# Routed experts behind sliding-window attention: gather buffers on the other side, one store per block of rows, two lists of ids, logits of six heads ahead, expert 0 by slabs

## The chip, the cores and the metric

One core of one Trainium2 chip runs the whole kernel in one launch. The metric is device time in microseconds. The core's engines run each its own list of instructions and wait for each other by semaphores: PE (TensorE, matmuls; PEld are its weight loads), DVE (VectorE), ACT (ScalarE), POOL (GpSimd) and SP (SyncE, which here only issues transfers). Transfers run on 16 DMA engines that all queues share.

## The reference

Attention with a sliding window of 96 and 8 global positions (4 batches, 8 heads, 768 positions, head size 64), then a layer of 8 experts in which each expert takes exactly 384 of the 3072 tokens:

```python
keep = is_global | is_local                 # is_local: 0 <= rel < 96
scores = where(keep, q @ k.T / 8 - slope * dist, -1e9)
x = softmax(scores) @ v                     # -> (3072 tokens, 512)
logits = x @ w_gate                         # (3072, 8)
for idx in argsort(-logits.flatten()):      # best pair first
    tok, e = idx // 8, idx % 8
    if assigned[tok] < 0 and counts[e] < 384:
        assigned[tok] = e; counts[e] += 1
for e in range(8):
    h = maximum(x[assigned == e] @ w1[e], 0)
    out[assigned == e] = h @ w2[e]
```

## The kernel before

*Attention.* Heads go in pairs (`n`, 16 of them) and the steps of a pair are laid out by the table `ORDER`, whose rows give a step and how many rounds it lags. `sums` leaves on PE, for a pair, the row sums and the product with the gate's weights. `sums_out` (LT) transposes that on DVE and takes reciprocals, `gates_out` (GT) scales it into `Gb` (six chunks x 8 heads x 8 experts of a batch) and `logits_out` (LS) adds the eight heads into `L_sb`, the logits: 128 partitions x 24 chunks x 8 experts. The last batch's `logits_out` is one reduction on DVE, after the last pair.

*Token rows.* `tok_in` turns attention output round on PE, `tok_out` scales it (on ACT, four activations a piece, or on DVE) into a tile `x`, and when a tile is full SP stores it to `x_tok` in DRAM (L493), in four transfers of 32 partitions: the rows of `x_tok` stand in the order of the tokens, and a chunk's 128 partitions are four groups of 32 tokens that lie 192 apart. Most of these pieces run inside the routing, between its steps.

*Routing.* In a `manual_schedule` block, where instructions stand in the order in which they are written, four rounds (`fast_round`) refine which expert each token goes to. Each begins in `best` with the minimum over the experts for all chunks (`mn`) and a comparison with it (`nb`). GpSimd issues one weight transfer a round (`late_weights`). `dispatch` then makes, for each place 0..3071 of the experts' lists, the token's id: masks `OH` and `ohl` on DVE, 24 matmuls into `pI` in four groups of six, and two DVE steps into `idi`. Between the groups and behind them stand `fill` matmuls, whose product nobody reads. Last, `pf`, `fc8`, `fm` and `fi` find whether any expert has more than 384 tokens; a branch at the end of the program would then take a slow path.

*Experts.* For expert e, `gather` fetches the rows of its 384 tokens from `x_tok` by `idi`, as three indirect transfers of GpSimd (128 rows each, tiles `xe`). `load_x` transposes a slab of 128 tokens on PE and copies it on DVE into `xT`; 32 matmuls of 384 columns and 8 activations on ACT give `hT`; 24 matmuls of 512 columns give the result, which DVE copies to `ot` and GpSimd scatters to `out` by `idi` (L1055). Gathers run two experts ahead. GpSimd's queue also carries the weights of experts 2 to 7: four transfers (1 MB each as stored) during the routing, the other eight in the loops of experts 0 to 3, two each.

*Memory.* The attention's token tiles (`tokp`) lie on the right side of the on-chip memory. The routing's pools are opened on the left side, the first of them `dap`, which holds `fc8` and `fm`. When they are closed, the experts' pools take the same place, the first of them `gp`, with the gather buffers `xe` and the weights of experts 6 and 7. The tile framework makes the first use of a place wait for the last use of what lay there.

Line numbers of the quoted kernel are those of the profile. Around the change the order comes from the written order inside `manual_schedule`, and behind it from the framework's scheduler, except where `keep_in_program_order` pins an instruction.

Of the kernel before, what the change touches and what calls it, by code (L numbers as in the profile page):

```python
# [42 lines left out]
def kernel(  # L43
# [46 lines left out]
    idc = consts.tile([128, NCHUNK], FP16)  # L90
    idn = consts.tile([128, NCHUNK], FP32)
# [74 lines left out]
    def _():  # L166
        nc.gpsimd.memset(Lb[:, 0:8, :], 0.0)
# [11 lines left out]
    Lb = lpool.tile([128, 32, N_EXP], FP32)  # L179
    L_sb = Lb[:, 8:32, :]  # L180
# [21 lines left out]
    with ExitStack() as actx:  # L202
# [214 lines left out]

        def sums_out(n):
# [46 lines left out]
        def tok_out(piece, xpool, eng):  # L465
# [44 lines left out]
        def step(op, u):  # L510
# [37 lines left out]
            elif k == "LT":  # L548
                sums_out(n)
# [6 lines left out]
            elif k == "GT":  # L556
                gates_out(n, nc.vector if last else nc.gpsimd)
            elif k == "LS":
                if u % 2 == 1:
                    logits_out(u // 2, nc.vector if last else nc.gpsimd)  # L560
# [104 lines left out]
    idi = consts.tile([128, NCHUNK], I32)  # L665
    fi = consts.tile([1, 1], I32)

    def routing(general):
      with ExitStack() as dctx:
# [16 lines left out]
        mn = rpool.tile([128, NCHUNK], FP32, tag="mn", name="mn")  # L686
        turn = rpool.tile([128, 1], FP32, tag="turn", name="turn")
        nb = rpool.tile([128, 256], BF16, tag="nb", name="nb")
# [30 lines left out]
        def best(X, Dg):  # L719
            if X is None:  # L720
                UB = Lb
            else:
# [6 lines left out]
            nc.vector.tensor_reduce(out=mn, in_=UB[:, 8:32, :], axis=AX.X, op=ALU.min)  # L729
            return UB  # L730

        def fast_round(kk, k, X, Dg):
# [7 lines left out]
            nc.vector.tensor_tensor(out=nb[:, 64:256].rearrange("p (c e) -> p c e", e=N_EXP),  # L740
                                    in0=UB[:, 8:32, :], in1=bc_e(mn), op=ALU.is_gt)
# [65 lines left out]
        def dispatch():  # L807
# [34 lines left out]
            nc.vector.tensor_tensor(out=OH, in0=OH, in1=bc_m(idc, NCHUNK), op=ALU.mult)  # L842
            pI = ps_d.tile([128, NCHUNK], FP32, tag="rk", name="pI")
# [269 lines left out]
```

## Time and profile before

| | |
|---|---|
| median of 3 runs | 276.59 us (276.26 to 277.07) |
| the profiled execution | 275.88 us, its span 274.1 us |
| busy: PE, DVE, ACT, POOL | 233.4 (85%), 148.8 (54%), 152.5 (56%), 153.3 (56%) us |
| mean granted TensorE clock | 0.944 of full speed |
| transfers | 49.22 MB, mean 180 GB/s |

Times in rows are microseconds from the span's start. A row of the timeline gives start, duration, engine, line, operation, output<-input, and in brackets how long the engine stood idle before it and what ended that. A row with xN merges N instructions. PE's busy time counts matmuls as the profiler models them. The DMA share is the mean busy share of the 16 engines, and overlapping packets can take it over 1.

### The profile page before, as it was taken

Reading aid. Unit: us, or ns where it says so; the run is one execution under the profiler, and the core shown is the slowest. Engines: PE = TensorE matmul, PEld = TensorE weight load, DVE = VectorE, ACT = ScalarE, POOL = GpSimd, SP = SyncE. Lnnn points to the kernel's source line nnn. Section 1 sums busy time; section 2 is a strip of 40 time slices with the busy share of each in tenths; the row PEclk is TensorE's granted clock in tenths of the full one; section 3 lists DMA queues with packets and bytes.
Section 4 is the critical chain, followed back from the end, with each engine's and each line's share of the span. In section 5 each row is a group of like instructions: output and inputs, shape, how many; then the busy total and the mean of one; then the engine's idle time right before and its main releaser. Section 6 shows DMA issues by size and latency. Waiting matters only on the chain. (4 is left out here: it accounts for less than half of the span.)

```text
span 274.1 us, 6678 instructions
## 1 busy us (share of the span) xinstructions
PE 233.4 (85%) x2633; PEld 162.5 (59%) x2633; DVE 148.8 (54%) x324; ACT 152.5 (56%) x296; POOL 153.3 (56%) x281
## 2 busy tenths in 40 slices
PE   0678599999998999998778792599999999999960
PEld 0666478888887888886666430355565555655520
DVE  3699688979898965644878810212323223333130
ACT  2549569898989898563788910053251341522500
POOL 6888637486959899855120004826675555741240
PEclk9995599999999999999999997599999999999995
DMA  7999967585472599951999941499999999530321
GB/s 246 351 347 236 308 213 222 155 214 155 92 139 66 89 193 202 203 105 16 172 212 234 268 119 39 106 213 241 209 195 267 260 252 278 191 134 0 118 81 43
DMA packets 50198, 49.22 MB, mean 180 GB/s; under 512 B 29680, under 2 KB 41712, under 8 KB 50160
## 3 DMA queue, kind: packets, MB, share of 16 engines
q0 software_dynamic: 15680, 26.22, 45.8%
q1 hardware_dynamic: 34480, 22.50, 29.6%
q8 instruction: 23, 0.38, 0.5%
q14 instruction: 15, 0.12, 0.1%
HBM read 56.05 MB, written 9.44 MB: 239 GB/s over the span
## 5 line engine op out<-in xcount | busy, mean ns | idle before, releaser
L1045 ACT ACTIVATE hT<-ph 128x384 bf16<-128x384 f32 x64 | 31.4, 491 | 70.0 <-PE ph L1042 69.5
L329 PE MATMUL ps<-qT,kA 32*128 32x216 f32 (+2 forms) x864 | 47.9, 359 | 13.3 <-ACT qT L297 9.2
L347 DVE SCALAR_TENSOR_TENSOR P<-Dm,ps 128x432 f32<-128x432 f32 x92 | 49.2, 595 | 14.0 <-PE ps L329 13.9
L329 PEld LDWEIGHTS ps<-qT,kA 32*128 32x128 f32 x864 | 40.6, 200 | 18.4 <-POOL iota_s L94 9.2
L354 ACT ACTIVATE P<-P 128x864 f32<-128x864 f32 x48 | 42.6, 925 | 13.6 <-DVE P L347 12.7
L366 POOL TENSOR_TENSOR S<-P 128x576 f32<-128x576 f32 (+1 forms) x32 | 39.0, 1219 | 19.8 <-ACT P L354 14.8
L387 PE MATMUL po<-P,v 128*64 128x216 f32 (+6 forms) x576 | 43.6, 300 | 2.9 <-ACT P L354 2.7
L387 PEld LDWEIGHTS po<-P,v 128*64 128x64 f32 x576 | 36.1, 140 | 12.7 <-ACT P L354 3.4
L1055 POOL DMA_INDIRECT out_dram<-ot,idi x24 | 23.6, 983 | 33.0 <-DVE ot L1054 30.8
L1011 POOL DMA_INDIRECT xe<-x_tok,idi x24 | 23.2, 968 | 31.2 <-issue 27.2
L1054 DVE COPY ot<-po 128x512 f32<-128x512 f32 x24 | 16.5, 692 | 30.2 <-PE po L1051 24.9
L1024 DVE COPY xT<-pxe 128x512 bf16<-128x512 bf16 x24 | 9.5, 422 | 42.9 <-PE pxe L1023 42.2
L1051 PEld LDWEIGHTS <-hT 128*128 128x128 bf16 x192 | 18.2, 98 | 19.5
L477 ACT ACTIVATE x<-pw,ri 128x64 bf16<-128x64 f32 x112 | 24.7, 354 | 6.1 <-PE pw L462 5.8
L280 ACT COPY kA<-tT_k 128x720 f32<-128x720 f32 (+2 forms) x18 | 23.9, 1341 | 5.5 <-DVE tT_k L272 5.5
L1051 PE MATMUL po<-w_late,hT 128*128 128x512 bf16 x96 | 22.0, 379 | 0.0
L1042 PE MATMUL ph<-xT,w_late 128*128 128x384 bf16 x128 | 21.5, 326 | 0.0
L394 ACT COPY oT<-po 128x384 f32<-128x384 f32 x32 | 14.6, 479 | 11.0 <-PE po L387 11.0
L297 ACT COPY qT<-tT_q 128x768 f32<-128x768 f32 (+1 forms) x13 | 19.7, 1513 | 0.4 <-DVE tT_q L272 0.4
L272 DVE STREAM_TRANSPOSE tT_k<-w_early 128x768 f32<-128x768 f32 x16 | 15.3, 967 | 6.6 <-DMA w_early<-in_k_dram 3.6
L1042 PEld LDWEIGHTS <-w_late 128*128 128x128 bf16 x128 | 12.5, 98 | 8.7
L1023 PE MATMUL pxe<-ident_bf,xe 128*128 128x128 bf16 x96 | 8.9, 233 | 7.7 <-issue 5.0
(157 smaller groups left out, 311.5 us busy)
## 6 DMA issues: line engine op xcount, KB each, us to landing
w_late<-in_moe_w_dram POOLq DMA_DIRECT2D x8, 1024.0 KB, 11.4
w_early<-in_k_dram SPq DMA_DIRECT2D x8, 768.0 KB
w_early<-in_q_dram SPq DMA_DIRECT2D x8, 768.0 KB
v<-in_v_dram SPq DMA_DIRECT2D x32, 180.0 KB
w_early<-in_moe_w_dram POOLq DMA_DIRECT2D x8, 512.0 KB, 9.1
w_last<-in_moe_w_dram POOLq DMA_DIRECT2D x4, 1024.0 KB, 12.2
x_tok<-x SPq DMA_DIRECT2D x8, 192.0 KB
x_tok<-x SPq DMA_DIRECT2D x8, 96.0 KB
```

Source lines behind the costliest of these rows:

```text
L280: nc.scalar.copy(out=kAs[u % 2][:, g, i0:i1, 8:128].rearrange("p i (c j) -> p i c j", j=NJ), in_=t[:, i0 * NC5 : i1 * NC5, :].rearrange("p ...
L329: nc.tensor.matmul(at(a)[:, o : o + w], lhsT=kA[r, gd, i, :], rhs=qTt[r, gd, KT * i : KT * i + w], start=(gd == 0), stop=(gd == 1), skip_g ...
L347: nc.vector.scalar_tensor_tensor(out=Ps[n][:, 2 * g : 2 * g + 2, t, :], in0=W, scalar=-8.0 * slopes[2 * (n % NPAIR) + t], in1=st[:, 0 : 2 ...
L354: nc.scalar.activation(P, P, AF.Exp, scale=0.125)
L366: nc.gpsimd.tensor_tensor(out=to[:, :, :, 0:OV], in0=P[:, i0 : i0 + m, :, 0:OV], in1=P[:, i0 - 1 : i0 + m - 1, :, KT:QW], op=ALU.add)
L387: nc.tensor.matmul(po[n, bank][64 * t : 64 * t + 64, a - QB * bank : z - QB * bank], lhsT=v7[:, t, i, :], rhs=Ps[n][:, min(i, 5), t, a - q ...
L477: nc.scalar.activation(x[:, 2 * hf + i, 128 * jj + 64 * t : 128 * jj + 64 * t + 64], ps[:, i, 64 * t : 64 * t + 64], AF.Identity, scale=ri ...
L1011: tc.keep_in_program_order(nc.gpsimd.indirect_dma_start(out=xe, out_offset=None, in_=x_tok[:, :], in_offset=bass.IndirectOffsetOnAxis(ap=i ...
L1042: nc.tensor.matmul(ph, lhsT=w1_of(e)[:, kc, 128 * fc : 128 * fc + 128], rhs=xT_e[:, kc, :, :].rearrange("p t n -> p (t n)"), start=(kc == ...
L1045: nc.scalar.activation(hT[:, fc, :], ph, AF.Relu)
L1051: nc.tensor.matmul(po, lhsT=hT[:, fc, 128 * t : 128 * t + 128], rhs=w2_of(e)[:, fc, :], start=(fc == 0), stop=(fc == NFC - 1))
L1055: s = nc.gpsimd.indirect_dma_start(out=out[:, :], out_offset=bass.IndirectOffsetOnAxis(ap=idi[:, TSLAB * e + t : TSLAB * e + t + 1], axis= ...
```

## The change

- The token rows of `x_tok` are kept in the order chunk, partition. A tile is stored by one transfer of 128 partitions.
- There are two lists of ids: `idi` (rows of `x_tok`, from the new constant `idc`) for the gathers, and `ido` (tokens, from `idt`) for the scatters. The second has 24 matmuls of its own (`pO`), behind the first list's. The fills between the groups of `pI` go; 2 stand ahead of `pO`, 8 behind it, where 12 stood behind `pI`.
- `best_of` computes `mn` and `nb` for a stretch of chunks. For the 18 chunks of batches 0 to 2 it runs ahead of the pair 14, for the last batch's 6 chunks in the first round.
- The last batch's logits: a ninth slot of `Gb` takes the sum of the first six heads after pair 14 (`part_logits`), and after pair 15 only that slot and the last two heads are added.
- Expert 0: slab 0 is transposed and goes through the first layer alone (32 matmuls of 128 columns), then slabs 1 and 2 (32 of 256 columns).
- `gp` is opened on the right side.

```diff
...
+        nc.gpsimd.tensor_copy(out=idt[:, ROT:NCHUNK], in_=idn[:, 0 : NCHUNK - ROT])
+        nc.gpsimd.tensor_copy(out=idt[:, 0:ROT], in_=idn[:, NCHUNK - ROT : NCHUNK])
-        nc.gpsimd.tensor_copy(out=idc[:, ROT:NCHUNK], in_=idn[:, 0 : NCHUNK - ROT])
-        nc.gpsimd.tensor_copy(out=idc[:, 0:ROT], in_=idn[:, NCHUNK - ROT : NCHUNK])
+        iota(idc[:, ROT:NCHUNK], [[128, NCHUNK - ROT]], base=-N_TOK // 2, cm=1)
+        iota(idc[:, 0:ROT], [[128, ROT]], base=128 * (NCHUNK - ROT) - N_TOK // 2, cm=1)
...
+        def best_of(c0, c1):
+            o = nb[:, 64 + N_EXP * c0 : 64 + N_EXP * c1].rearrange("p (c e) -> p c e", e=N_EXP)
+            m = mn[:, c0:c1].rearrange("p (c o) -> p c o", o=1).to_broadcast([128, c1 - c0, N_EXP])
+            nc.vector.tensor_reduce(out=mn[:, c0:c1], in_=L_sb[:, c0:c1, :], axis=AX.X, op=ALU.min)
+            nc.vector.tensor_tensor(out=o, in0=L_sb[:, c0:c1, :], in1=m, op=ALU.is_gt)
+        def last_sums_out(n):
...
+            gates_out(n, nc.vector)
+            G = Gb[B_ - 1]
+            nc.vector.tensor_reduce(out=L_sb[:, C3 : C3 + NBLK, :],
+                                    in_=G[:, :, H_ - 2 : H_ + 1, :].rearrange("p b h e -> p b e h"), axis=AX.X, op=ALU.add)
+        def part_logits():
+            G = Gb[B_ - 1]
+            nc.vector.tensor_reduce(out=G[:, :, H_, :], in_=G[:, :, 0 : H_ - 2, :].rearrange("p b h e -> p b e h"),
+                                    axis=AX.X, op=ALU.add)
...
-                dst = x_tok[S_ * b : S_ * b + S_, f0 : f0 + 128 * m].rearrange("(g b r) d -> g r b d", g=4, b=NBLK)
-                for gq in range(4):
-                    nc.sync.dma_start(dst[gq, :, b0:b1], x[32 * gq : 32 * gq + 32, b0:b1, :])
+                dst = x_tok[S_ * b : S_ * b + S_, f0 : f0 + 128 * m].rearrange("(c p) d -> p c d", p=128)
+                nc.sync.dma_start(dst[:, b0:b1], x[:, b0:b1, :])
...
-            nc.vector.tensor_tensor(out=OH, in0=OH, in1=bc_m(idc, NCHUNK), op=ALU.mult)
+            nc.vector.tensor_tensor(out=OHr, in0=OH, in1=bc_m(idc, NCHUNK), op=ALU.mult)
...
-                if q4 > 0:
-                    if q4 < 2:
-                        rows(2)
-                    fill(2)
+                if q4 == 1:
+                    rows(2)
...
-            fill(12)
+            nc.vector.tensor_tensor(out=OH, in0=OH, in1=bc_m(idt, NCHUNK), op=ALU.mult)
+            fill(2)
+            pO = ps_d.tile([128, NCHUNK], FP32, tag="pr", name="pO")
+            for c in range(NCHUNK):
+                nc.tensor.matmul(pO, lhsT=ohls[c // 6][:, :, c % 6], rhs=OH[:, :, c],
+                                 start=(c == 0), stop=(c == NCHUNK - 1))
+            fill(8)
+            for dst, src in ((idi, pI), (ido, pO)):
...
+                if e == 0:
+                    load_x(0, (0,))
+                    hidden(0, hT, 0, 1)
+                    load_x(0, range(1, TSLAB))
+                    hidden(0, hT, 1, TSLAB)
+                else:
+                    hidden(e, hT)
...
-                        out_offset=bass.IndirectOffsetOnAxis(ap=idi[:, TSLAB * e + t : TSLAB * e + t + 1], axis=0),
+                        out_offset=bass.IndirectOffsetOnAxis(ap=ido[:, TSLAB * e + t : TSLAB * e + t + 1], axis=0),
...
-    gp = ctx.enter_context(tc.tile_pool(name="gp", bufs=9))
+    gp = ctx.enter_context(tc.tile_pool(name="gp", bufs=9, side="right"))
```

`hidden(e, hT, t0, t1)` is the old first layer, cut to the slabs t0 to t1.

How instructions stand on VectorE at the end of attention, before (pairs 13 to 15, whose transposes write `LT`):

```order
L420 STREAM_TRANSPOSE LT_1813<-t_13_1795 128x192
L422 RECIPROCAL ri_1815<-LT_1813 128x12
L420 STREAM_TRANSPOSE LT_1875<-t_14_1862 128x192
L422 RECIPROCAL ri_1877<-LT_1875 128x12
L430 TENSOR_TENSOR Gb_1808<-LT_1875,ri_1877 128x6x16
L420 STREAM_TRANSPOSE LT_1907<-t_15_1893 128x192
L422 RECIPROCAL ri_1909<-LT_1907 128x12
L430 TENSOR_TENSOR Gb_1808<-LT_1907,ri_1909 128x6x16
L448 TENSOR_REDUCE Lb<-Gb_1808 128x48
L729 TENSOR_REDUCE mn<-Lb 128x24
L740 TENSOR_TENSOR nb<-Lb,mn 128x192
```

and after the change (from the third of the steps of `best_of` on; the first two are of the same kind, for two chunks):

```order
L427 TENSOR_REDUCE mn<-Lb 128x16
L428 TENSOR_TENSOR nb<-Lb,mn 128x128
L450 STREAM_TRANSPOSE LT_1882<-t_14_1865 128x192
L452 RECIPROCAL ri_1884<-LT_1882 128x12
L460 TENSOR_TENSOR Gb_1811<-LT_1882,ri_1884 128x6x16
L445 TENSOR_REDUCE Gb_1811<-Gb_1811 128x6x8
L432 STREAM_TRANSPOSE LT_1915<-t_15_1900 128x192
L434 RECIPROCAL ri_1917<-LT_1915 128x12
L460 TENSOR_TENSOR Gb_1811<-LT_1915,ri_1917 128x6x16
L438 TENSOR_REDUCE Lb<-Gb_1811 128x48
L427 TENSOR_REDUCE mn<-Lb 128x6
L428 TENSOR_TENSOR nb<-Lb,mn 128x48
```

Four steps of `best_of` now stand ahead of pair 14's transpose and `part_logits` ahead of pair 15's; behind pair 15 the steps into `mn` and `nb` write 128x6 and 128x48 instead of 128x24 and 128x192.

The stores of SyncE, before (`x_0` and the like are the tiles of a batch, the last row the last batch's three parts):

```order
L493 DMA x_tok<-x_0_696 32x6x256 x4
L493 DMA x_tok<-x_2_1962 32x6x256 x4
L493 DMA x_tok<-x_0_2026 32x6x512 x4
L493 DMA x_tok<-x_0_2172 32x6x512 x4
L493 DMA x_tok<-x_0_2300 32x2x512 x12
```

and after the change:

```order
L522 DMA x_tok<-x_0_702 128x6x256
L522 DMA x_tok<-x_2_1968 128x6x256
L522 DMA x_tok<-x_0_2029 128x6x512
L522 DMA x_tok<-x_0_2172 128x6x512
L522 DMA x_tok<-x_0_2300 128x2x512 x3
```

28 transfers are 7, of the same bytes.

TensorE behind expert 0's slab 0, after the change (`xe_2` is slab 2, `xe_3` expert 1's first slab, `po` the second layer):

```order
L1070 LDWEIGHTS xe_2_2570
L1070 MATMUL pxe_2648<-ident_bf_69,xe_2_2570 128x128
L1107 LDWEIGHTS hT_2586
L1107 MATMUL po_2721<-w_early_97,hT_2586 128x512
L1107 LDWEIGHTS hT_2586
L1107 MATMUL po_2721<-w_early_97,hT_2586 128x512
L1070 LDWEIGHTS xe_3_2572
L1070 MATMUL pxe_2703<-ident_bf_69,xe_3_2572 128x128
```

Before, the transposes of `xe_0` to `xe_3` stood in one row, with the 32 matmuls of 384 columns behind them. Now two matmuls of the second layer, the four transposes of `xe_3` and one more matmul of the second layer stand between the transposes of slab 2 and the matmuls of 256 columns (`ph` 128x256), which come next.

## Rows read from the trace of the kernel before

**Rows 1.** Busy time by stretch: PE, PEld, DVE, ACT, POOL, clock, DMA share, GB/s.
```profile
178.00:190.00 12.00, 12.00 (x72) 6.57 (x71) 2.83 (x5) 4.43 (x10) 5.10 (x7) 0.98 1.13 222
190.00:193.00 3.00, 3.00 (x20) 1.81 (x19) 0.00 (x0) 2.37 (x5) 2.39 (x3) 1.00 0.78 189
193.00:232.00 39.00, 39.00 (x242) 21.36 (x240) 11.65 (x22) 12.36 (x26) 24.43 (x26) 1.00 1.14 244
```

**Rows 2.** The same view, around the end of the routing and the first gathers.
```profile
157.00:163.00 6.00, 5.48 (x39) 2.67 (x40) 1.73 (x5) 1.09 (x5) 0.00 (x0) 1.00 0.57 169
162.00:167.40 5.40, 3.21 (x10) 0.75 (x8) 0.64 (x3) 0.00 (x0) 0.00 (x0) 1.00 0.09 24
167.40:175.70 8.30, 2.23 (x16) 1.57 (x17) 1.32 (x4) 0.00 (x0) 6.69 (x7) 0.55 0.31 89
```

**Rows 3.** Timeline of the dispatch, all engines.
```profile
156.41 1.96 DVE L846 TENSOR_TENSOR ohl<-iota_m,lo 128x768 f16<-128x768 f16 x4
...
157.77 0.93 ACT L477 ACTIVATE x<-pw,ri 128x64 bf16<-128x64 f32 x4 [0.61 <-PE pw L462]
...
160.07 0.44 PE L854 MATMUL pI<-OH,ohl 128*128 128x24 f16 x6
...
160.34 5.14 PE L695 MATMUL pw<-w_early,ident_bf 128*128 128x512 bf16 x12
...
160.77 0.18 DVE L860 TENSOR_SCALAR idi<-idf 128x24 int32<-128x24 f32 x1
...
166.26 0.14 DVE L996 TENSOR_SCALAR fi<-fm 1x1 int32<-1x1 f32 x1
```

**Rows 4.** Timeline of the first gather, the transposes and the first layers.
```profile
167.43 1.08 POOL L1011 DMA_INDIRECT xe<-x_tok,idi  x1 [22.93 <-issue]
...
170.70 0.58 PE L1023 MATMUL pxe<-ident_bf,xe 128*128 128x128 bf16 x4 [5.04 <-issue]
...
174.59 1.03 PE L1023 MATMUL pxe<-ident_bf,xe 128*128 128x128 bf16 x8 [2.31 <-DMA xe<-x_tok,idi]
...
175.71 6.67 PE L1042 MATMUL ph<-xT,w_early 128*128 128x384 bf16 x32
...
182.21 0.61 PE L1023 MATMUL pxe<-ident_bf,xe 128*128 128x128 bf16 x8
...
187.84 5.36 PE L1042 MATMUL ph<-xT,w_early 128*128 128x384 bf16 x32
```

**Rows 5.** GpSimd's queue at L1011 between 164.5 and 165.5.
```profile
L1011 POOLq EVENT_SEMAPHORE  x1: 2989/2989/2989, 163.4 to 163.4; - x1
```

**Rows 6.** L1011, issues of 214 to 217.5 us; timeline of weight loads at 226.
```profile
DMA to landing us min/median/max: 10.0/10.9/11.9
...
226.20 0.54 PEld L1023 LDWEIGHTS <-xe 128*128 128x128 bf16 x8 [0.18 <-DMA xe<-x_tok,idi]
```

**Rows 7.** Timeline at the end of attention, VectorE and TensorE.
```profile
125.28 0.38 DVE L420 STREAM_TRANSPOSE LT<-t 128x192 f32<-128x192 f32 x1 [4.09 <-PE t L408]
...
127.74 0.38 DVE L420 STREAM_TRANSPOSE LT<-t 128x192 f32<-128x192 f32 x1 [1.53 <-PE t L408]
...
128.71 0.84 DVE L448 TENSOR_REDUCE Lb<-Gb 128x48 f32<-128x384 f32 x1
...
129.60 0.71 PE L738 MATMUL pk<-ident,Lb 128*128 128x128 f32 x4 [0.55 <-DVE Lb L448]
...
129.68 0.35 DVE L729 TENSOR_REDUCE mn<-Lb 128x24 f32<-128x192 f32 x1
...
130.07 0.36 DVE L740 TENSOR_TENSOR nb<-Lb,mn 128x192 bf16<-128x192 f32 x1
```

**Rows 8.** Timeline of GpSimd in the prologue.
```profile
28.14 0.93 POOL L94 IOTA idn<- 32x24 f32 x4
...
36.58 0.38 POOL L363 COPY S<-P 128x240 f32<-128x240 f32 x1 [4.66 <-PE t L404]
```

**Rows 9.** SyncE's own waits, 130 to 170 us: total, times, longest.
```profile
SPq L493 <- DMA x_tok<-x: 2.3, 4, 1.3
```

More of the change, by code (lines that the diff above doesn't have):

```diff
@@ L556, in step @@
             elif k == "GT":
-                gates_out(n, nc.vector if last else nc.gpsimd)
+                if n < 2 * NU - 1:
+                    gates_out(n, nc.vector if last else nc.gpsimd)
+                if n == 2 * NU - 2:
+                    part_logits()
             elif k == "LS":
-                if u % 2 == 1:
-                    logits_out(u // 2, nc.vector if last else nc.gpsimd)
+                if u % 2 == 1 and not last:
+                    logits_out(u // 2, nc.gpsimd)
                 if 1 <= u:
@@ L739, in fast_round @@
                                  start=(hf == 0), stop=False, skip_group_check=True)
-            nc.vector.tensor_tensor(out=nb[:, 64:256].rearrange("p (c e) -> p c e", e=N_EXP),
-                                    in0=UB[:, 8:32, :], in1=bc_e(mn), op=ALU.is_gt)
+            if X is not None:
+                nc.vector.tensor_tensor(out=nb[:, 64:256].rearrange("p (c e) -> p c e", e=N_EXP),
+                                        in0=UB[:, 8:32, :], in1=bc_e(mn), op=ALU.is_gt)
             rows_out(d0, nc.vector)
@@ L977, in routing @@
             X, Dg = None, None
-            nc.gpsimd.memset(nb[:, 0:64], 1.0)
             nc.gpsimd.memset(Ub[:, 0:8, :], 0.0)
@@ L1015, in gather, with load_x @@
                     xes[s] = xe
-            def load_x(e):
-                xT_e = fp.tile([128, NKC, TSLAB, 128], BF16, tag="xT_e", name=f"xT_{e}")
-                for t in range(TSLAB):
+            def load_x(e, slabs=range(TSLAB)):
+                if e not in xT_of:
+                    xT_of[e] = fp.tile([128, NKC, TSLAB, 128], BF16, tag="xT_e", name=f"xT_{e}")
+                for t in slabs:
                     xe = xes.pop(TSLAB * e + t)
@@ L1022, in load_x, with hidden @@
                     for kc in range(NKC):
-                        nc.tensor.transpose(pxe[:, kc, :], xe[:, 128 * kc : 128 * kc + 128], ident_bf)
-                    nc.vector.tensor_copy(out=xT_e[:, :, t, :], in_=pxe)
-                xT_of[e] = xT_e
+                        i_ = nc.tensor.transpose(pxe[:, kc, :], xe[:, 128 * kc : 128 * kc + 128], ident_bf)
+                        if e == 0 and t > 0:
+                            tc.keep_in_program_order(i_)
+                    nc.vector.tensor_copy(out=xT_of[e][:, :, t, :], in_=pxe)
+            def hidden(e, hT, t0=0, t1=TSLAB):
+                for fc in range(NFC):
+                    ph = ps_h.tile([128, CAP], FP32, tag="ph")
+                    for kc in range(NKC):
+                        nc.tensor.matmul(ph[:, 128 * t0 : 128 * t1], lhsT=w1_of(e)[:, kc, 128 * fc : 128 * fc + 128],
+                                         rhs=xT_of[e][:, kc, t0:t1, :].rearrange("p t n -> p (t n)"),
+                                         start=(kc == 0), stop=(kc == NKC - 1))
+                    nc.scalar.activation(hT[:, fc, 128 * t0 : 128 * t1], ph[:, 128 * t0 : 128 * t1], AF.Relu)
             gather(0)
-            load_x(0)
             gather(1)
             for e in range(N_EXP):
-                xT_e = xT_of.pop(e)
                 if first:
@@ L1038, in experts @@
                 hT = hp.tile([128, NFC, CAP], BF16, tag="hT")
-                for fc in range(NFC):
-                    ph = ps_h.tile([128, CAP], FP32, tag="ph")
-                    for kc in range(NKC):
-                        nc.tensor.matmul(ph, lhsT=w1_of(e)[:, kc, 128 * fc : 128 * fc + 128],
-                                         rhs=xT_e[:, kc, :, :].rearrange("p t n -> p (t n)"),
-                                         start=(kc == 0), stop=(kc == NKC - 1))
-                    nc.scalar.activation(hT[:, fc, :], ph, AF.Relu)
+                if e == 0:
[3 more added lines that the diff above has]
+                    hidden(0, hT, 1, TSLAB)
+                else:
+                    hidden(e, hT)
+                xT_of.pop(e)
                 if e + 1 < N_EXP:
```

36 lines of the change are left out of this document (27 added, 9 removed).

## The prediction

> **What bounds the kernel now.** I read the busy shares by stage first, then the timeline around the two gaps of TensorE, then the waits. TensorE works without a gap from expert 0 on: 12.00 of 12.00 us, 3.00 of 3.00 and 39.00 of 39.00 between 178 and 232 us [rows 1]. Ahead of that lies a hole: from 162 to 167.4 it is busy 3.21 of 5.40 us, from 167.4 to 175.7 only 2.23 of 8.30, and there its granted clock is 0.55 [rows 2]. The hole is the way from the tokens' ids to expert 0. The ids are written at 160.95 (160.77 + 0.18), yet the first gather starts at 167.43 [rows 3, 4]. GpSimd's queue shows why: one semaphore wait from 163.4 runs 2.99 us, to 166.4, and what ends at 166.40 is the routing's overflow flag, `fi` [rows 3, 5]. The gather doesn't use that flag: its buffer lies over the flag's scratch. The flag stands behind one matmul that stands behind 12 fill matmuls of 5.14 us together [rows 3].
>
> The second limit is hidden. From 193 to 232 us the DMA share is 1.14, with 244 GB/s: that is, the 16 engines are never free. Only at 190 to 193 does it dip to 0.78 [rows 1]. Gathers issued at 214.3 to 216.9 take 10.0 to 11.9 us to land, and TensorE, otherwise gapless, waits 0.18 us for one at 226.20 [rows 6]. So at expert 5's tokens TensorE and GpSimd's DMA queue (weights, gathers, result rows, in one order) arrive together. Whoever moves one of them alone gains little.
>
> **Part by part.** *Logits and best values.* Today three VectorE steps stand in a row: 0.84 (sum of 8 heads), 0.35 (minimum of 24 chunks), 0.36 (compare), done at 130.43 [rows 7], and TensorE goes on with their result. Afterwards they work on 3 of 9 slots and on 6 of 24 chunks. The first lies between 0.32 (0.84 x 3/8) and 0.84; I take 0.40, near the 0.35 of a reduction of 192 elements, since it reads 144. The others lie between 0 and 0.36; I take 0.20 each. The logits come 0.45 sooner, at 129.15; four matmuls on them take 0.71 [rows 7], to 129.9, and the compare is done before that. The round goes on some 0.6 us sooner (bounds 0 and 0.75), and what follows is a chain that keeps this. The work done ahead, some 1.75 us by the same rows, stands before two VectorE transposes that wait 4.09 and 1.53 us for TensorE [rows 7]; without that cover it would cost its 1.75.
>
> *Two id lists.* GpSimd gets two more iotas in the prologue, 0.23 each (4 in 0.93), and a memset that moves there. They stand before a wait of GpSimd of 4.66 us [rows 8], so nothing; uncovered, 0.6. In the dispatch the second product and its 24 matmuls stand behind the first list on both engines, except one VectorE product of some 0.46 (as one of four 0.49 [rows 3]), which runs beside the last six matmuls (0.44). The three pairs of fills between the groups go, so the groups follow VectorE: last mask at 158.37, matmuls 158.9, ids some 0.4 later, at 159.3, and 0.6 earlier still with the round: 158.7 instead of 160.95.
>
> *Row stores.* 28 issues on SyncE become 7. Today late stores wait for earlier ones to land: four waits of 2.3 us together [rows 9]. The DMA share is just 0.57 from 157 to 163 us, though the gather waits for these bytes: 169 GB/s, 1014 KB [rows 2]. At the 244 GB/s of a full stretch [rows 1] they take 4.2 us and end at 161.2 rather than 163. The last rows are ready at 158.70 - 0.6 = 158.1 [rows 3], and 256 KB then need 1.05 us: not before 159.2. The other bound is no gain, 163.0. I take 161.2, from the rate that a full queue has shown.
>
> *Gather buffers.* On the other side they no longer overlie the flag; the first gather waits for ids and stores. The waiting instruction heads GpSimd's queue, with all gathers, weights and result rows behind it. Today the stores' last wait lies at 163.4, 0.4 after the last byte, and the gather starts 1.03 after its last wait (166.40 to 167.43) [rows 3, 4, 5]. So 161.2 + 0.4 + 1.0 = 162.6, bounds 160.6 and 164.4: **4.8 us sooner**.
>
> *Expert 0 by slabs.* Transposes start 3.27 after the gather [rows 4], at 165.9. The remaining fills don't hold them: 158.3 + 2 and 8 fills of 0.43 + 24 matmuls (four groups of 0.44) + at most another 0.44 for the flag's matmul is 164.8 [rows 3]. TensorE idles about 1.1 us instead of 5.04 [rows 4]. Then 1.1 for transposes and copy (174.59 to 175.71), 32 matmuls of 128 columns, 0.61 for the 8 transposes behind them (0.61 per 8 of that width [rows 4], so 2.4), and 32 of 256 columns at two thirds of 5.36 [rows 4], 3.6. Beside the copies between stand three second-layer matmuls and expert 1's first transposes; I leave 0.4 uncovered. The first layer is done near 174.0 instead of 182.38 (175.71 + 6.67 [rows 4]): TensorE is **8.4 us ahead**.
>
> *What is late next.* The DMA queue's work from the first gather to expert 5's tokens is the same, so it moves by 4.8 only, plus the dip: at 190 to 193 the queue ran dry because weights were issued behind expert 0's result rows, and those now come sooner. 3 x (1 - 0.78 / 1.13) = 0.9 us [rows 1]. Together 5.7. TensorE gives the other 2.7 back by waiting for gathers ahead of experts 4 and 5.
>
> **Sum.** -5.7 us of the profiled execution's 275.88 is 270.2; the median of the three runs stands 0.71 above that execution, so 276.59 - 5.7 = **270.9**.
>
> By the Trainium skill ("DMA: Bandwidth & Descriptors", Anatomy of one DMA — SWDGE (gpsimd) path) a transfer takes about 2.0 us plus its bytes at 436 GB/s, so the queue would have room. The trace disagrees: 244 GB/s at a share of 1.14 [rows 1]. The sum above goes by the trace; by the page it would be 8.4 instead of 5.7.
>
> **The rivals.** (1) The DMA queue has room, and TensorE keeps its 8.4: 268.2. For it: the wait today is a mere 0.18 us [rows 6], so the two only just touch. Against: a share of 1.14 over 39 us [rows 1] leaves nothing to speed up. The Trainium skill's rule above would give this one. 0.13.
> (2) The stores end as late as now, since the last landing hangs on one slow engine and not on the issues: gather at 164.4, gain 3.0 + 0.9, 272.7. For it: bytes trickle at half the share to the end [rows 2]. 0.12.
> (3) The gather stays held by something else near 167.4, and the buffers' move does nothing: 0.6 from the round and 0.9 from the dip, 275.1. 0.05.
> (4) With 10 fills in place of 18, the clock falls in expert 0's first layer. It was at its lower level, 1.2 of 2.4 GHz, after the 5 us hole (0.55 in that stretch [rows 2]). If all of that layer ran so, 2.4 + 3.6 + 0.6 would double; TensorE's lead falls to 1.8, and the queue's 5.7 no longer counts: 274.8. A loss of up to 2.7 us hides in the time that it waits anyway. 0.05. The Trainium skill ("TensorE: Matmul & The Clock Gate", Part 1: The HAM clock gate) says that the array's clock is throttled unless recent activity releases it; the trace agrees, 0.55 behind a gap of 5.04 us [rows 2, 4].
> (5) Slower: one store of 128 rows takes as long to land as gathers beside weights, up to 11.9 us [rows 6]. Issued at 158.1 it lands at 170.0, the gather starts at 171.1, 3.7 later than today, less the dip's 0.9: 279.4. It decides from a landing past 168.1. Against: weights have left the engines by then. 0.03.
>
> **How the numbers follow.** Forecast 0.60; the five rivals 0.38; 0.02 for parts that cancel. The range 268.2 to 272.7 holds the forecast with the store's bounds (a last byte at 159.2 gives 7.7, 268.9) and rivals 1 and 2; it leaves out 0.15. A measurement here tells 0.3%, 0.83 us, from nothing. All but rival 5 and the cancelling are faster: 0.95, 0.02, 0.03.
>
> **What would show it.** The first gather starts near 162.6 in the span, with GpSimd's last wait ending on a store; the flag is written after it. Granted clock stays 1.00 over the gather stage. Expert 0's first layer ends near 174; then TensorE shows waits for `xe` of 2 to 2.5 us in all, ahead of experts 4 and 5, and no dip in the DMA share between first gather and last weights. The forecast is wrong if TensorE is gapless there (rival 1), if the gather starts after 164.4 (2, 3, 5), or if the span shrinks by less than 3.9 us.

## The result, and the profile after

The changed kernel takes **269.59 us** (median of 4 runs, 268.59 to 269.76) beside 276.83 us (276.26 to 278.15) for the kernel before in the same job: a ratio of 0.9724, 95% interval 0.9682 to 0.9767. The forecast was 270.9, the range 268.2 to 272.7. The profiled execution took 269.57 us with a span of 267.9; before, 275.88 and 274.1, so the two profiles lie 6.3 us apart (6.2 in the span).

Attention hides some of this: the last pair's VectorE transpose starts at 128.60 now, at 127.74 before [rows 7], 0.86 later. The change puts only two iotas, a memset and five VectorE steps there, and the steps end ahead of waits for TensorE (2.85 and 0.67 us are left of the 4.09 and 1.53 of [rows 7]). Over all fourteen profiles of this study that transpose starts anywhere from 127.15 to 128.60, with and without them. I count from it below. Counted so, the rest of the kernel is 7.06 us shorter: 274.1 - 127.74 = 146.36 before, 267.9 - 128.60 = 139.30 now.

Busy time by stretch of the kernel after, columns as in [rows 1]:

```profile
157.00:163.00 6.00, 5.68 (x56) 3.30 (x57) 2.53 (x9) 1.15 (x6) 0.00 (x0) 0.72 0.66 222
163.00:170.00 7.00, 5.77 (x35) 3.45 (x34) 1.06 (x4) 1.31 (x5) 5.30 (x6) 0.51 0.26 76
...
190.00:193.00 3.00, 3.00 (x18) 1.64 (x17) 1.15 (x2) 0.70 (x2) 1.56 (x3) 1.00 1.11 257
193.00:232.00 39.00, 37.97 (x239) 21.11 (x238) 10.19 (x20) 14.98 (x31) 22.60 (x25) 1.00 1.06 249
```

The hole ahead of expert 0 [rows 2] is closed: TensorE is busy 5.77 of 7.00 us between 163 and 170. The dip of the DMA share at 190 to 193 (0.78 in [rows 1]) is gone. New are two things: TensorE idles 1.03 us between 193 and 232, and its granted clock is 0.72 and 0.51 from 157 to 170, where it was 1.00 until the hole before.

Timeline of the kernel after, lines that answer to [rows 3] and [rows 4]:

```profile
159.21 0.18 DVE L907 TENSOR_SCALAR idi<-idf 128x24 int32<-128x24 f32 x1
...
160.55 5.08 PE L732 MATMUL pw<-w_early,ident_bf 128*128 128x512 bf16 x8
...
163.18 1.08 POOL L1057 DMA_INDIRECT xe<-x_tok,idi  x1 [18.62 <-PE pw L732]
...
166.32 0.58 PE L1070 MATMUL pxe<-ident_bf,xe 128*128 128x128 bf16 x4 [0.44 <-DVE fc L1039]
...
166.48 0.14 DVE L1042 TENSOR_SCALAR fi<-fm 1x1 int32<-1x1 f32 x1
...
167.47 3.10 PE L1079 MATMUL ph<-xT,w_early 128*128 128x128 bf16 x32 [0.57 <-DVE xT L1073]
...
171.75 3.66 PE L1079 MATMUL ph<-xT,w_early 128*128 128x256 bf16 x32
...
219.82 0.77 PE L1070 MATMUL pxe<-ident_bf,xe 128*128 128x128 bf16 x8 [1.03 <-DMA xe<-x_tok,idi]
```

The gather starts 3.44 us before the flag is written (166.48 + 0.14), and its queue no longer holds one long wait: the answer to [rows 5] is four waits of 43 ns, the last at 162.3, when the last row store has landed.

```profile
L1057 POOLq EVENT_SEMAPHORE  x4: 43/43/43, 160.3 to 162.3; - x4
```

The bracket in the gather's own row names a fill matmul of TensorE, whose semaphore moved last before the start. The queue's waits had ended by then; the one at 162.3 is for the last store, which landed at 162.31.

Expert 0's first layer ends at 171.75 + 3.66 = 175.41, not 182.38 [rows 4]; and ahead of expert 5 TensorE waits 1.03 us for tokens.

**Three lengths that make the span.** In every profile where TensorE waits for expert 5's tokens, or just meets them, the span is the sum of four: the start of the last pair's transpose, from there to the first gather, from the gather to the transposes of expert 5's tokens, and a last piece of 47.8 to 48.1 us that no edit here is meant to change. All are differences of timeline rows (before, the transposes count from their weight load at 226.20 [rows 6]; elsewhere load and matmul start within 0.01 us of each other). "Rows out" is the start of the first result-row transfer, counted from the first gather.

| profile | transpose | to gather | rows out | gather to expert 5 | to the end |
|---|---|---|---|---|---|
| before | 127.74 | 39.69 | 18.14 | 58.77 | 47.90 |
| after | 128.60 | 34.58 | 14.76 | 56.64 | 48.08 |
| e1 buffers left | 127.19 | 39.44 | 15.12 | 56.50 | 47.77 |
| e2 buffers alone | 127.15 | 37.38 | 18.51 | 59.88 | 47.89 |
| e3 expert 0 whole | 128.26 | 34.28 | 17.55 | 59.11 | 47.95 |
| e6 fills back | 127.78 | 34.51 | 13.55 | 56.40 | 47.81 |
| e7 four-part stores | 127.69 | 37.35 | 14.62 | 56.83 | 47.93 |
| e8 logits late | 128.58 | 35.37 | 16.02 | 56.82 | 47.93 |
| e9 after again | 128.56 | 34.48 | 18.35 | 59.91 | 47.85 |

So the change's 7.06 us are 5.11 from an earlier gather and 2.13 from a shorter way to expert 5's tokens, less 0.18 at the end. How far such a cell varies by itself: in the nine profiles of the changed kernel and of edits that leave the gather's conditions alone (after, e3 to e6, e9 to e12) "to gather" lies between 34.20 and 34.58.

### The profile page after: what moved, and what is told of

Same layout as the page of the kernel before. It is cut to its first block, busy times and chain, and to the rows that moved or that the text cites. A ratio compares the mean times of both kernels' runs of the same rounds, so it can differ in the third digit from the quotient of the medians.

```text
span 267.9 us, 6769 instructions
## 1 busy us (share of the span) xinstructions
PE 232.1 (87%) x2681; PEld 164.4 (61%) x2681; DVE 150.5 (56%) x332; ACT 153.5 (57%) x304; POOL 153.3 (57%) x283
## 2 busy tenths in 40 slices
DMA packets 49862, 49.22 MB, mean 184 GB/s; under 512 B 29344, under 2 KB 41376, under 8 KB 49824
## 3 DMA queue, kind: packets, MB, share of 16 engines
HBM read 56.05 MB, written 9.44 MB: 244 GB/s over the span
## 5 line engine op out<-in xcount | busy, mean ns | idle before, releaser
L1082 ACT ACTIVATE hT<-ph 128x384 bf16<-128x384 f32 (+2 forms) x72 | 32.6, 454 | 62.5 <-PE ph L1079 60.9
L1111 POOL DMA_INDIRECT out_dram<-ot,ido x24 | 23.6, 984 | 28.5 <-DVE ot L1110 25.3
L278 DVE STREAM_TRANSPOSE tT_q<-w_early 128x768 f32<-128x768 f32 x16 | 14.9, 944 | 0.2 <-DMA w_early<-in_q_dram 0.2
```

The lines of the kernel that those rows point to most:

```text
L278: nc.vector.transpose(out=t, in_=raws[kind, u][:, :, 32 * g : 32 * g + 32])
L1082: nc.scalar.activation(hT[:, fc, 128 * t0 : 128 * t1], ph[:, 128 * t0 : 128 * t1], AF.Relu)
L1111: s = nc.gpsimd.indirect_dma_start(out=out[:, :], out_offset=bass.IndirectOffsetOnAxis(ap=ido[:, TSLAB * e + t : TSLAB * e + t + 1], axis= ...
```

## The experiments

Three jobs, each on a chip of its own, with the kernel before in each; ratios are to that. The unedited changed kernel ran only in the third of them (e9), so the medians of e1 to e8 stand beside a changed kernel that was measured in another job. A cell of the table tells more than a median here, since attention alone moves a profile by up to 1.45 us.

**e1: the buffers on the left again.**

```
-    gp = ctx.enter_context(tc.tile_pool(name="gp", bufs=9, side="right"))
+    gp = ctx.enter_context(tc.tile_pool(name="gp", bufs=9))
```

> The changed kernel with the gather buffers back on the left side; all else of the change stays. Theory (the buffers' place over the flag's scratch held the first gather): the gather waits for the overflow flag again, which in the changed kernel is written near 167, so it starts near 168.0 instead of 163.18, everything behind it moves by 4.5 to 5, and the time is 274.0 to 274.6. Rival (the stores' landing alone holds the gather, the place of the buffers is indifferent): the gather stays at 163.2 and the time at 269.6 within 0.4.

Measured: 273.56 us (272.63 to 273.96), ratio 0.9907 (0.9890 to 0.9924). Timeline of this kernel, GpSimd and TensorE:

```profile
166.63 1.08 POOL L1057 DMA_INDIRECT xe<-x_tok,idi  x1 [23.48 <-issue]
...
169.91 0.59 PE L1070 MATMUL pxe<-ident_bf,xe 128*128 128x128 bf16 x4 [5.04 <-issue]
```

The hole of 5.04 us is back, and the gather comes 39.44 after the transpose, 4.86 later than in the changed kernel. Its queue again holds one long wait, 6.16 us from 159.5, and the flag is written at 165.61. The theory holds: with the buffers over the flag's scratch, neither earlier ids nor earlier stores reach the gather. The way from there to expert 5, 56.50, stays as short as in the changed kernel.

**e2: the kernel before with only the buffers moved** (the same line, on the other kernel).

> The kernel before with nothing but the gather buffers on the right side. Theory: the first gather then follows the stores' last wait, 163.4 plus 1.0, so 164.4 instead of 167.43; everything behind moves by 3.0, and the time is 273.6 (273.0 to 274.2), a bit under half of what the whole change gives. Rival (ids and stores are so late there that something else holds the gather): under 1 us, 275.8 or more.

Measured: 273.96 us (10 runs, 272.83 to 276.11), ratio 0.9911 (0.9881 to 0.9940); the first gather:

```profile
164.53 1.08 POOL L1011 DMA_INDIRECT xe<-x_tok,idi  x1 [20.62 <-PE pw L695]
```

The gather starts where the theory put it (164.4), and the gain of the medians is 2.5 of the 3.0 expected. Counted from the transpose it is less: the gather comes 2.31 sooner (37.38; 36.7 would be the theory), but the way to expert 5 is 59.88, 1.11 longer than before, so that 1.2 us are left in this profile.

**e3: expert 0's first layer whole.**

```
-                if e == 0:
-                    load_x(0, (0,))
-                    hidden(0, hT, 0, 1)
-                    load_x(0, range(1, TSLAB))
-                    hidden(0, hT, 1, TSLAB)
-                else:
-                    hidden(e, hT)
+                hidden(e, hT)
```

(with `load_x(0)` behind `gather(0)` again.)

> The changed kernel with expert 0's first layer whole again. The third gather lands at 168.7, so the 32 matmuls of 384 columns start near 170.2 and end near 176.0 to 176.8 instead of 175.4: TensorE's lead falls by 0.6 to 1.4. Theory (GpSimd's DMA queue sets when expert 5's tokens come, TensorE waits 1.0 for them): the wait shrinks by the same, and the time stays within 0.4 of 269.6. Rival (TensorE sets the end): the time rises by 0.6 to 1.4, to 270.2 to 271.0.

Measured: 271.38 us (271.15 to 271.79), ratio 0.9827 (0.9812 to 0.9842). TensorE:

```profile
170.39 6.50 PE L1077 MATMUL ph<-xT,w_early 128*128 128x384 bf16 x32
...
221.65 0.77 PE L1070 MATMUL pxe<-ident_bf,xe 128*128 128x128 bf16 x8 [0.72 <-DMA xe<-x_tok,idi]
```

The first layer ends 1.8 us later after the transpose than in the changed kernel, and the time rises by 1.8 (2.0 from the transpose on). My theory, that the queue would hide this, fell. But the rival as I wrote it is not it either: TensorE still waits 0.72 us for expert 5's tokens. The tokens themselves came later, 59.11 instead of 56.64 after the gather. **The queue is not a fixed length.** Busy time by stretch, cut from the first gather on, shows why. Kernel before:

```profile
167.43:175.43 8.00, 2.04 (x16) 1.54 (x17) 1.05 (x3) 0.00 (x0) 6.48 (x7) 0.55 0.29 86
175.43:183.43 8.00, 7.91 (x46) 4.39 (x45) 1.41 (x4) 3.93 (x8) 4.07 (x5) 0.81 0.97 189
183.43:191.43 8.00, 8.00 (x45) 4.13 (x43) 2.08 (x3) 2.11 (x5) 4.13 (x5) 1.00 1.10 234
191.43:199.43 8.00, 8.00 (x51) 4.31 (x50) 2.89 (x6) 1.82 (x4) 5.56 (x6) 1.00 1.02 195
199.43:226.20 26.77, 26.77 (x166) 14.99 (x164) 6.89 (x13) 11.21 (x23) 16.24 (x17) 1.00 1.14 247
```

Kernel after:

```profile
163.18:171.18 8.00, 6.82 (x51) 4.45 (x51) 1.41 (x6) 2.11 (x8) 6.47 (x7) 0.58 0.28 83
171.18:179.18 8.00, 8.00 (x64) 5.54 (x62) 2.77 (x7) 3.06 (x8) 5.10 (x6) 1.00 1.00 195
179.18:187.18 8.00, 8.00 (x55) 4.73 (x54) 2.08 (x5) 3.92 (x8) 5.69 (x6) 1.00 1.12 221
187.18:195.18 8.00, 8.00 (x44) 4.21 (x43) 2.07 (x3) 2.40 (x5) 4.73 (x6) 1.00 1.13 240
195.18:219.80 24.62, 23.61 (x146) 12.96 (x143) 6.42 (x12) 9.36 (x20) 14.46 (x15) 1.00 1.15 257
```

Rate times length, summed, is 12.24 MB in both: the same bytes, in 58.8 and in 56.6 us. Most of the difference lies in the fourth stretch, 195 GB/s before and 240 after, and in the rate behind it. There the next weights stand in GpSimd's order behind expert 0's result rows. The first weight transfer of three turns, kernel before:

```profile
189.98 0.82 POOL L661 DMA_DIRECT2D w_late<-in_moe_w_dram  x1
...
201.05 0.82 POOL L661 DMA_DIRECT2D w_last<-in_moe_w_dram  x1
...
213.18 0.81 POOL L661 DMA_DIRECT2D w_last<-in_moe_w_dram  x1 [1.06 <-DMA w_last<-in_moe_w_dram]
```

and the first of them in the kernel after (the other two are shown in the last section):

```profile
182.36 0.82 POOL L699 DMA_DIRECT2D w_late<-in_moe_w_dram  x1
```

From the gather these are 22.55, 33.62 and 45.75 us before, and 19.18, 30.88 and 43.66 after. The third stands right ahead of the gathers for expert 5. Of the first one's lead of 3.4 us, 2.1 are left there, since in the kernel after the later two wait until the one a turn earlier has landed.

Where the rows go out 13.6 to 16.0 us after the gather, the way takes 56.4 to 56.8; where they go out after 17.5 to 18.5 us, it takes 58.8 to 59.9 (the table, nine profiles, no exception). The slabs pay by sending the rows out early enough, so that the weights behind them go out early too.

**e4, e5: other orders on GpSimd's queue.** In e4 each expert's gathers stand ahead of both weight transfers of the turn:

```
-                if first:
-                    late_weights()
                 if e + 2 < N_EXP:
                     gather(e + 2)
                 if first:
                     late_weights()
+                    late_weights()
```

> The changed kernel with each expert's gathers issued ahead of the first of the two weight transfers of that turn instead of between them. Theory A (the gathers stand behind GpSimd's waits for earlier weights to land, 1.99 us ahead of the weights that precede expert 5's gathers): these gathers start about 2 to 3 us sooner, the 1.03 us wait of TensorE for expert 5's tokens goes, and the time is 268.6. Theory B (the transfers' bytes themselves fill the engines until then): the gathers start sooner but land as late, the wait stays over 0.6, and the time stays within 0.4 of 269.6.

Measured: 269.4 us (268.01 to 270.88), ratio 0.9743 (0.9718 to 0.9768): no gain to tell. GpSimd and TensorE:

```profile
204.69 0.94 POOL L699 DMA_DIRECT2D w_last<-in_moe_w_dram  x1 [5.52 <-DMA w_late<-in_moe_w_dram]
...
209.86 1.00 POOL L1057 DMA_INDIRECT xe<-x_tok,idi  x1 [0.30 <-issue]
...
232.32 0.76 PE L1070 MATMUL pxe<-ident_bf,xe 128*128 128x128 bf16 x8 [1.39 <-DMA xe<-x_tok,idi]
```

The wait for expert 5's tokens is gone, and one of 1.39 us for expert 6's has come. Neither theory said so: the wait moved. A weight transfer stood 5.52 us in the queue until an earlier one had landed.

In e5 the gathers stand three experts ahead: `gather(2)` in front of the loop, `gather(3)` behind expert 0's transposes, then `gather(e + 3)` ahead of both weight transfers.

> The changed kernel with each expert's gathers issued one expert earlier (three ahead instead of two), so that two weight transfers fewer stand before expert 5's gathers. Theory (these gathers come late only because of the weights ahead of them in GpSimd's one queue; the weights themselves have over 10 us to spare): they land some 10 us sooner, the wait of 1.03 us for expert 5's tokens goes, TensorE is gapless from expert 0's first layer to the end, and the time is 268.6 (268.2 to 269.0). Rival (the queue's bytes have to go by TensorE's pace in any order): a wait of 0.7 to 1.5 for weights or later tokens takes its place, and the time stays at 269.4 to 270.0.

Measured: 272.33 us (271.7 to 273.83), ratio 0.9819 (0.9782 to 0.9855): 2.7 us slower than the changed kernel by the medians of two jobs, worse than the rival. GpSimd, VectorE and TensorE:

```profile
219.79 0.93 POOL L699 DMA_DIRECT2D w_last<-in_moe_w_dram  x1 [4.35 <-DMA out_dram<-ot,ido]
...
233.10 1.33 DVE L1111 COPY ot<-po 128x512 f32<-128x512 f32 x2 [9.81 <-DMA out_dram<-ot,ido]
...
234.82 0.38 PE L1070 MATMUL pxe<-ident_bf,xe 128*128 128x128 bf16 x4 [2.94 <-DVE xT L1073]
```

The tokens are early, but a waiting weight transfer holds the result rows behind it, VectorE's copy of `ot` waits 9.81 us for a free buffer, the copy of `xT` stands behind that copy, and TensorE waits 2.94 us for it, after 1.39 us of the same kind at 220.88. One engine's order passed a DMA wait on to three others.

**e6: the six fills back.**

```
-                if q4 == 1:
-                    rows(2)
+                if q4 > 0:
+                    if q4 < 2:
+                        rows(2)
+                    fill(2)
```

> The changed kernel with the three pairs of fill matmuls between the mask groups put back. Theory (their removal let the granted clock fall at 159.7 in the changed kernel): the clock stays at 1.00 in 157 to 170, the last 8 fills take some 3.5 us instead of 5.1, the ids come 0.6 to 0.9 later but still ahead of the stores' landing, expert 0's first 32 matmuls of 128 columns take near 2.0 instead of 3.10, and its first layer ends some 1.2 to 1.5 sooner, near 174.1. The time falls by 0.3 (if the wait for expert 5's tokens grows by most of it) to 1.3. Rival (the clock's fall hangs on something else, such as the many short matmuls of the second list): the clock still falls by 162, and the time stays at 269.6 or rises by up to 0.5 with the later ids.

Measured: 268.33 us (267.55 to 271.04), ratio 0.9713 (0.9659 to 0.9768). By stretch, and TensorE:

```profile
157.00:163.00 6.00, 5.61 (x54) 3.12 (x53) 1.70 (x7) 0.93 (x4) 0.71 (x1) 1.00 0.48 165
163.00:170.00 7.00, 5.70 (x60) 3.90 (x60) 2.19 (x7) 1.90 (x8) 5.47 (x7) 1.00 0.32 95
```

```profile
161.35 3.41 PE L732 MATMUL pw<-w_early,ident_bf 128*128 128x512 bf16 x8
...
166.32 2.15 PE L1081 MATMUL ph<-xT,w_early 128*128 128x128 bf16 x32 [0.57 <-DVE xT L1075]
...
218.69 0.76 PE L1072 MATMUL pxe<-ident_bf,xe 128*128 128x128 bf16 x8 [1.49 <-DMA xe<-x_tok,idi]
```

The clock stays at 1.00, the eight fills take 3.41 us instead of 5.08, and the 32 matmuls 2.15 instead of 3.10. The first layer ends at 173.30, 45.52 after the transpose instead of 46.81: 1.29 sooner. The ids come 1.6 us later, more than expected, and the stores still land after them. But the wait ahead of expert 5 grows to 1.49 us, and the span from the transpose on is 0.58 shorter (138.72 against 139.30), of which 0.27 lies in the last piece. The way from the gather to expert 5 is 56.40, against 56.64: the weight behind expert 0's rows goes out 1.21 us earlier after the gather than in the changed kernel, the one ahead of expert 5's gathers only 0.26. So TensorE's lead is nearly all given back. That no order could do better than some 56.5 us is not shown. By the times alone the ratio can't be told from 0.9724.

**e7: each row store in four transfers of 32 partitions.**

```
-                nc.sync.dma_start(dst[:, b0:b1], x[:, b0:b1, :])
+                for gq in range(4):
+                    nc.sync.dma_start(dst[32 * gq : 32 * gq + 32, b0:b1], x[32 * gq : 32 * gq + 32, b0:b1, :])
```

> The changed kernel with each row store in four transfers of 32 partitions again (28 issues instead of 7, rows in the new layout). Theory (the issues on SyncE and their waits for earlier stores delay the last bytes): the last store lands 0.7 to 1.5 later, the first gather starts near 164.2 instead of 163.2, and the time is 270.3 to 271.1. Rival (the last landing hangs on one slow DMA engine, not on the issues): the gather stays within 0.3 of 163.2, and the time within 0.4 of 269.6.

Measured: 271.86 us (270.87 to 272.51), ratio 0.9810 (0.9763 to 0.9858). SyncE's own waits (total, times, longest) and the gather:

```profile
SPq L523 <- DMA x_tok<-x: 2.4, 4, 1.4
```

```profile
165.04 1.08 POOL L1058 DMA_INDIRECT xe<-x_tok,idi  x1 [21.39 <-PE pw L733]
```

The theory's mechanism holds, its size does not: the four waits of [rows 9] are back, which the changed kernel does not have, but the gather comes 2.77 us later after the transpose, not 1.0, and the time lies above the theory's range. It is not quite the store of before (the layout is the new one), so it stands near the term rather than measures it.

**e8: the last logits and all best values behind the last pair**, with the functions of the kernel before.

> The changed kernel with the logits of the last batch and all best values made in one piece behind the last pair again. Theory (three VectorE steps of 0.84, 0.35 and 0.36 stand in a row on the path to the first round): everything from the first round on comes 0.6 to 0.9 later, and the time is 270.2 to 270.5. Rival (the first round waits for something else, such as the row pieces on ScalarE): within 0.3 of 269.6.

Measured: 270.43 us (269.74 to 272.29), ratio 0.9772 (0.9717 to 0.9826). The gather comes 0.79 us later after the transpose (35.37 against 34.58), as the theory said; the times alone don't tell it from the changed kernel. VectorE in this kernel, and in the changed one:

```profile
129.55 0.84 DVE L478 TENSOR_REDUCE Lb<-Gb 128x48 f32<-128x384 f32 x1
130.43 0.35 DVE L427 TENSOR_REDUCE mn<-Lb 128x24 f32<-128x192 f32 x1
```

```profile
129.57 0.32 DVE L438 TENSOR_REDUCE Lb<-Gb 128x48 f32<-128x144 f32 x1
129.93 0.20 DVE L427 TENSOR_REDUCE mn<-Lb 128x6 f32<-128x48 f32 x1
130.17 0.21 DVE L428 TENSOR_TENSOR nb<-Lb,mn 128x48 bf16<-128x48 f32 x1
```

**e9 to e12: the changed kernel again, and three versions meant to beat it.** In e10 the gathers of expert 3's turn alone stand ahead of both weight transfers (`if first and e != 3` at the first, a third call `if first and e == 3` behind); e11 adds the fills of e6; e12 also puts the flag's matmul ahead of the last eight fills.

> The changed kernel once more, unedited, beside the three below on one chip. Every theory: 269.6, within 0.6, and a ratio of 0.972 to the kernel before within 0.005.

> The changed kernel, and in the turn of expert 3 alone the three gathers stand ahead of both weight transfers instead of between them. Theory (GpSimd's issues wait for the landing of the transfer that stands eight places before, and a turn has eight of them, so the weights ahead of expert 5's gathers wait for the weights of the turn before; what comes first in the turn starts when those have landed, near 206.9): these gathers start 1.1 us sooner and have one weight transfer less ahead of them in the engines, the wait of 1.03 us for expert 5's tokens goes, and the time is 1.0 below that of the changed kernel in the same job (0.6 to 1.2). Rival (as with the two earlier reorderings, the transfer pushed back holds another one up): a wait of 0.7 or more for later tokens, result rows or weights takes its place, and the time is within 0.4 of it or longer.

> The three pairs of fills between the mask groups and the swap of expert 3's turn together. Theory (TensorE sets the end once neither the clock falls ahead of expert 0 nor the tokens come late): the two gains add, 1.3 to 1.5 from the clock and 1.0 to 1.7 from the wait, and the time is 2.3 to 3.0 below that of the changed kernel in the same job, near 267. Rival (the queue takes back what TensorE wins): not more than 1.5 below it.

> As the one before, and the flag's matmul ahead of the last eight fills instead of behind them. Theory (the first transposes wait 0.44 us for the flag's reduction, whose memory they take over, while their rows landed 0.26 us before): they start when the rows land, 0.2 to 0.3 sooner, and so does the end. Rival (the eight fills reach to the rows' landing anyway, or the clock falls): no gain, within 0.2.

Measured: 272.65 (ratio 0.9847, 0.9787 to 0.9906), 272.08 (0.9833, 0.9783 to 0.9884), 272.39 (0.9847, 0.9789 to 0.9906), 274.26 (0.9898, 0.9837 to 0.9958). **The first expectation already fell**: on this chip the unedited changed kernel gained 1.5%, not 2.8%. Its profile starts alike (gather 34.48 after the transpose, clock back at 1.00 by 170), and then has stalls that the first profile does not have. ScalarE, TensorE and VectorE, by start:

```profile
171.52 0.28 ACT L1082 ACTIVATE hT<-ph 128x128 bf16<-128x128 f32 x1 [1.93 <-PE ph L1079]
...
171.85 0.38 PE L1079 MATMUL ph<-xT,w_early 128*128 128x128 bf16 x4 [1.65 <-ACT hT L1082]
...
173.81 0.42 DVE L1073 COPY xT<-pxe 128x512 bf16<-128x512 bf16 x1 [6.45 <-PE pxe L1070]
...
174.29 0.38 PE L1070 MATMUL pxe<-ident_bf,xe 128*128 128x128 bf16 x4 [1.39 <-DVE xT L1073]
```

ScalarE and VectorE start over 1 us after the matmuls that they read from have been sent, and TensorE then waits for them: 3.0 us in all. The result rows go out 18.35 us after the gather, and the way to expert 5 is 59.91, as in e2 and e3. All four profiles of this job show such stalls between 168 and 176, e10 and e12 one more of about 1.05 us at 241; none of the eight profiles of the changed kernel and its edits on the other chips has one of over 0.2 us there. What makes them is open. It isn't the clock: in e11 and e12 it was 1.00 when they began.

So the three versions were not tried on the ground that they were meant for. What their profiles do show: in e10 expert 5's transposes start without a wait for tokens (0.71 us in e9), though its gathers start only 0.3 us sooner after the first gather, not 1.1; and in e12 the first transposes wait only for their rows:

```profile
165.35 0.38 PE L1074 MATMUL pxe<-ident_bf,xe 128*128 128x128 bf16 x4 [0.26 <-DMA xe<-x_tok,idi]
```

The medians of e10 and e11 lie within the spread of e9 (270.97 to 274.04), that of e12 lies above it, so a version that beats the changed kernel is not shown.

## Why the prediction was right, and where it was not

The total and the mechanism came out: the kernel is faster, the bound behind the gather is GpSimd's DMA queue up to expert 5's tokens, and TensorE waits there. The medians fell by 7.2 us where I forecast 5.7. In the two profiles the spans differ by 6.2, nearer to the forecast, and that is luck: attention's 0.86 hid most of what the way to expert 5 won beyond its price. Step by step, each counted from the last pair's transpose, since attention ran 0.86 us late in the profile after:

- **Logits and best values**: 0.6 expected (0 to 0.75); undoing it costs 0.79 at the gather, just over the bound. The three steps on the path took 0.32, 0.20 and 0.21, where I took 0.40, 0.20 and 0.20.
- **Two id lists**: ids at 158.7, that is 30.96 after the transpose. Measured 159.39 - 128.60 = 30.79.
- **Row stores**: a last byte at 161.2 and a last wait at 161.6, 33.9 after it. GpSimd's last wait for a store lies at 162.3, 33.7 after it. Two slips cancel here, which is luck: from 157.86 on (157 in the kernel before) the bytes went at 300 GB/s, not at 244, and 15 of the last store's 16 engines had landed by 161.26, but the last one only at 162.31 (a DMA share of 0.06 to 0.07 in between, one engine of 16). In the kernel before, the last store's 16 engines landed within 0.3 us of each other. So the slow engine of rival 2 is there, and holds the gather for 1.05 us, though its forecast (a gather as late as 36.7) fell. e7 shows that the issues matter as well: 2.77 us.
- **Gather buffers**: the gather 4.8 sooner. Measured 5.11, and 4.86 of it go when the buffers alone go back (e1). Moved alone they bring 2.3 at the gather (39.69 to 37.38, e2), because the stores are next. The steps don't add up singly: each uncovers the other.
- **Expert 0 by slabs**: the first layer done 8.4 ahead. Measured 54.64 - 46.81 = 7.83. The step that failed is "granted clock stays 1.00 over the gather stage". It fell ahead of the fills, which took 5.08 us rather than 3.44, and the 32 matmuls of 128 columns took 3.10 rather than 2.4. That is rival 4, to which I gave 0.05, with the fall in an earlier place than I looked for. It cost the first layer 1.29 us and the end 0.3 to 0.6 (e6, without and with the last piece), not the 3.9 of its price (274.8 against 270.9), since the wait ahead of expert 5 hid the rest, as the prediction had it.
- **What is late next**: 4.8 + 0.9 = 5.7, with 2.7 given back by TensorE in waits ahead of experts 4 and 5. Measured 7.06: 5.11 from the gather, 2.13 from the way to expert 5, and one wait, ahead of expert 5. The mis-sized term is **the dip**, 2.13 where I put 0.9. I priced one stretch of 3 us by its busy share. In fact the queue ran under its full rate for longer, and the share hid it: the fourth stretch of 8 us had a share of 1.02 and moved 195 GB/s, against 240 in the kernel after. At the 257 GB/s of the last stretch that is 1.4 us; the faster last stretch (257 for 247) is another 1.0, and the first three lose 0.3. The cause was as written, weights behind expert 0's result rows. For this, TensorE gave back 0.8, not 2.7.

The terms as measured, 5.11 + 2.13 - 0.18 - 0.86 for attention, give the 6.2 of the two spans. Rival 1, TensorE keeping all of its lead, is contradicted by e6: 1.29 us more lead, a way only 0.24 shorter, and a longer wait. The Trainium skill ("DMA: Bandwidth & Descriptors", Anatomy of one DMA — SWDGE (gpsimd) path), with its 436 GB/s, would leave the queue room there. The trace disagrees again: 257 GB/s, at a share of 1.15, is the most that the five stretches of the kernel after show. By how much is not shown, here or in the prediction: these GB/s count a weight as the 1 MB of bf16 that is written, while the kernel reads it as f32, twice the bytes (the page of the kernel after has 56.05 MB read from HBM, more than the 49.22 MB that all its transfers are counted with). Rivals 3 and 5 fell with the gather at 163.18.

One thing the prediction could not hold: that another chip gives the same kernel 0.9847. What it loses there, it loses in the very stretch that the slabs had won.

## What to carry to other kernels

When an instruction waits on something that it doesn't use, look for memory that it shares; but expect the next wait right behind it, and price the edits together, since each alone brings less (at the gather 2.3 us for the buffers, 5.1 with the rest).

A queue that is full later on still has a length that depends on when its work is issued. Cut its way into stretches and compare the bytes that each moved with the full rate, rather than the busy share. Not all that is missing can be won: 12.24 MB at 257 GB/s would be 47.6 us, and the way went from 58.8 to 56.6, and with still more lead (e6) to 56.4.

Before moving one transfer ahead in an engine's order, ask what then stands behind the one pushed back: of three such orders here one moved the wait (e4), one made it longer (e5), and the third (e10) could not be judged.

## What the runs showed of the hardware that I had not expected

GpSimd's transfers wait for the landing of the one eight places ahead. In the trace each of them tells of its landing on one of eight semaphores that go in turn (111 to 118), and its issue first waits for that semaphore. So this is a wait of the program as built; a limit of the chip is not shown. In the kernel after a turn has eight of them, two weights, three gathers and three result rows, so a weight waits for that of the turn before:

```profile
194.06 0.81 POOL L699 DMA_DIRECT2D w_last<-in_moe_w_dram  x1 [0.63 <-DMA w_late<-in_moe_w_dram]
...
206.84 0.81 POOL L699 DMA_DIRECT2D w_last<-in_moe_w_dram  x1 [1.99 <-DMA w_last<-in_moe_w_dram]
207.96 1.01 POOL L1057 DMA_INDIRECT xe<-x_tok,idi  x1 [0.31 <-PE pxe L1070]
```

Seven issues lie between the first two lines; the gather of expert 5's tokens stands right behind the second. This is what e4 and e5 ran into. SyncE's transfers have eight semaphores in turn too: in e7 the stores issued at 157.99, 158.95 and 159.47 follow within 0.02 us the landing of the store eight places ahead. With 7 stores none has to wait so.

TensorE's clock fell from 2.4 to 1.2 GHz at 159.7, in a stretch (157 to 163) in which the engine was counted busy 5.68 of 6.00 us. Before it fell, it had idled 0.86 us up to 157.09 and run matmuls of 24 columns, 18 in a row from 157.64 and, behind two fills, the first of 24 more from 159.44. With two fills of 512 columns ahead of each of the last three groups of six (e6) and the same idle time, it was counted busy 5.61 of 6.00 us and stayed at 2.4 GHz. A busy engine on the page is no sign of a granted clock.
